# Attention scores of three row blocks per stretch instead of two, in a fused attention and MoE kernel

## The chip, the cores and the metric

The kernel runs on one core of a Trainium2 chip. The metric is device time in microseconds (us) of one execution. The kernel before was timed three times: median 813.93 us, lowest 813.37, highest 815.35.

The engines of a core are named as the profile names them: PE (matrix products; PEld is its loading of weights), DVE (vector work), ACT (exponentials and copies with a scale), POOL (vector work without access to the accumulation banks), SP (here it only issues transfers). PE writes into eight accumulation banks, each of 128 rows by 512 fp32 numbers, from which DVE and ACT read.

## The reference

`x` of 2048 rows by 640 is normalized row by row to `xn`. It feeds an attention with 32 heads of 192 over the last 512 rows of a cache, and a small MoE that picks two rows; the result is `x + s * g`.

```python
def _A_ref(x, k_cache, v_cache, wq, wo):
    ...
    q = (lambda x, *d: x.transpose(*d))((x @ wq).reshape(B, Sq, Hq, Dh), 0, 2, 1, 3)
    ...
    scores = jnp.einsum("bhqd,bhkd->bhqk", q, k) * (Dh ** -0.5)
    p = _softmax(scores, axis=-1)
    o = jnp.einsum("bhqk,bhkd->bhqd", p, v)
    return (lambda x, *d: x.transpose(*d))(o, 0, 2, 1, 3).reshape(B, Sq, Hq * Dh) @ wo
...
xn = _layernorm(x, axis=-1)
s = _A_ref(xn, A_k_cache, A_v_cache, A_wq, A_wo)
g = _silu(_B_ref(xn, B_w_r, B_w_gate, B_w_up, B_w_down))
return x + s * g
```

`_B_ref` finds the two rows with the largest `xn @ w_r`, runs them through a gated feed-forward layer, and adds the results to `xn` at these rows.

## The kernel before

**Loops.** The 32 heads are taken in 8 groups of 4, a group as two couples of heads (`pr`). The 2048 rows are taken in 4 blocks of 512 (`t5`). A step `i` is one group, one row block, one couple of heads; there are 64 steps. A step has four row blocks of 128, and one row block of 128 for one couple of heads is called a pair below: 256 pairs in all. The main loop runs over 128 stretches `k`, each with two pairs (`quad`, L310).

**One stretch**, in the order in which the code writes it; the code fixes each engine's order itself, and every engine works through its own list in that order, waiting where data or a buffer is missing:

- `quad`: scores of two pairs, four banks. A head's 192 columns are contracted in a full part of 128 rows and a rest of 64 rows. The four full products come first (L321, L322), then the rests (L327, L328), two at a time in the two halves of PE's rows.
- `row_max` (L339): DVE takes the negated maximum of each of the four score tiles.
- `exps` (L346): ACT takes the exponentials into `pexp`, with the row sums; SP then transposes `pexp` into `pT` by a transfer, once for both pairs (L352).
- `q_item` (L288): the q products of a later step in five matmuls of 512 columns each, copied out by ACT with a scale (L293). There are three per step.
- `o_item`: P V of stretch `k - 2`, eight matmuls of 192 columns per pair (L364), scaled by DVE with the reciprocal of the sums (L378). After the second pair SP transposes `o_sb` into `oT` (L382).
- `w_item`: the product of a 128-row block's o with wo for the group, six matmuls of 512 columns (L411) and six of 128 (L413), into the two banks of `w_ps`; DVE adds all 640 columns to `s_acc` (L419).
- `mid` and `bg`: lists of further work by stretch. They hold the MoE (products with `w_r` at L588, gates at L773 and L774), the normalization, and SP's loads of the next group.

The first 12 stretches and the last one are written out as token lists (`FIRST`, `LAST`), where each token is one of the items above.

**Banks.** `ps_sc` has four for scores, `ps_f` two for q, P V and small MoE products, `ps_w` two for `w_ps`.

**Rings.** `pexp` has 2 buffers, `pT` 4, `o_sb` 2, `oT` 3, each for the two pairs of a stretch.

**Transfers.** Nearly all are issued by SP in order; an issue that waits for its data holds up the ones behind it.

Of the kernel before, what the change touches and what calls it, by code (L numbers as in the profile page):

```python
# [21 lines left out]
def kernel(ctx, tc, A_x, A_k_cache, A_v_cache, A_wq, A_wo, B_x, B_w_r, B_w_gate, B_w_up, B_w_down, out):  # L22
    nc = tc.nc
# [44 lines left out]
    p_pool = pool("p", 2)  # L68
    pT_pool = pool("pT", 4)
    o_pool = pool("o", 2)  # L70
    oT_pool = pool("oT", 3)
# [10 lines left out]
    s_acc = big.tile([P, NTB, D], FP32, name="s_acc")  # L82

# [58 lines left out]
    warm_ps = ps_w.tile([P, W], FP32, name="warm_ps", tag="w_ps")  # L142
# [106 lines left out]
    def k_turn(copies):  # L249

        grp[0]["kT"] = kT_pool.tile([P, PAIRS, NJ, 3, P], BF16, name="kT")
        tp = ps_w.tile([P, NJ * 3, P], BF16, name="tp_k", tag="w_ps")
        kp = grp[0][("k", 0)].rearrange("p j h d -> p (j h d)")
        kT = grp[0]["kT"][:, 0].rearrange("p j c t -> p (j c) t")
        step = NJ * 3 // len(copies)
        for c in range(NJ * 3):
            nc.tensor.transpose(out=tp[:, c, :], in_=kp[:, c * P:(c + 1) * P], identity=ident)
        for q, copy in enumerate(copies):
            cs = slice(q * step, (q + 1) * step)
            copy(out=kT[:, cs], in_=tp[:, cs])  # L260
# [10 lines left out]
    NH = 2 * NS  # L271
    qT_of = {}
    pT_of = {}
    l_of = {}
    pe_of = {}
    o_of = {}
    oT_of = {}
# [32 lines left out]
    def quad(k):  # L310
        i, hf = divmod(k, 2)
        g, t5, pr = steps[i]
        qT = qT_of[i]
        kT = grp[g]["kT"]
        kp = kT[:, pr]
        tiles = []
        for u in range(2):
            ssl = slice((2 * hf + u) * P, (2 * hf + u + 1) * P)
            s0 = ps_sc.tile([P, W], FP32, name="s0", tag="sc")
            s1 = ps_sc.tile([P, W], FP32, name="s1", tag="sc")  # L320
            nc.tensor.matmul(s0, lhsT=qT[:, 0, ssl], rhs=kp[:, :, 0, :], start=True, stop=False)  # L321
            nc.tensor.matmul(s1, lhsT=qT[:, 2, ssl], rhs=kp[:, :, 2, :], start=True, stop=False)  # L322
            tiles.append((s0, s1))
        for u in range(2):
            ssl = slice((2 * hf + u) * P, (2 * hf + u + 1) * P)
            s0, s1 = tiles[u]
            nc.tensor.matmul(s0, lhsT=qT[0:64, 1, ssl], rhs=kp[0:64, :, 1, :], start=False, stop=True)  # L327
            nc.tensor.matmul(s1, lhsT=qT[64:128, 1, ssl], rhs=kp[64:128, :, 1, :], start=False, stop=True)  # L328
        return tiles
# [3 lines left out]
    def row_max(k, tiles, c):  # L333
        if c == 0:
            nm_of[k] = small.tile([P, 4], FP32, name="nm")
            l_of[k] = small.tile([P, 4], FP32, name="lsum", bufs=6)
            pT_of[k] = pT_pool.tile([P, 2, 2, NJ, P], BF16, name="pT")
            pe_of[k] = p_pool.tile([P, 2, 2, W], BF16, name="pexp")
        nc.vector.tensor_reduce(out=nm_of[k][:, c:c + 1], in_=tiles[c // 2][c % 2], axis=AX.X, op=ALU.max, negate=True)  # L339

    def exps(k, u, tiles):
        pexp = pe_of[k]
        nm = nm_of[k]
        for hh in range(2):
            c = 2 * u + hh
            nc.scalar.activation(out=pexp[:, u, hh, :], in_=tiles[u][hh], func=ACT.Exp, bias=nm[:, c:c + 1],  # L346
                                 scale=1.0, accum_out=l_of[k][:, c:c + 1])
        if k >= NH - 2:
            nc.sync.dma_start_transpose(out=pT_of[k][:, u].rearrange("p h j t -> p (h j) t"),
                                        in_=pexp[:, u].rearrange("p h k -> p (h k)"))  # L350
        elif u == 1:
            nc.sync.dma_start_transpose(out=pT_of[k].rearrange("p u h j t -> p (u h j) t"),  # L352
                                        in_=pexp.rearrange("p u h k -> p (u h k)"))

    def recip(k):
        nc.vector.reciprocal(out=l_of[k], in_=l_of[k])

    def o_products(k, u):
        i, hf = divmod(k, 2)
        g, t5, pr = steps[i]  # L360
        o_ps = f_tile([P, 2, Dh], FP32, "o_ps")
        for hh in range(2):
            for j in range(NJ):
                nc.tensor.matmul(o_ps[:, hh, :], lhsT=pT_of[k][:, u, hh, j, :], rhs=grp[g]["v"][:, 2 * pr + hh, j, :],  # L364
                                 start=(j == 0), stop=(j == NJ - 1))
        return o_ps

    def o_scaled(k, u, o_ps, act=False):
        i, hf = divmod(k, 2)
        g, t5, pr = steps[i]  # L370
        if u == 0:
            o_of[k] = o_pool.tile([P, 2, 2, Dh], BF16, name="o_sb")
        o_sb = o_of[k]
        if act:
            for hh in range(2):
                nc.scalar.activation(out=o_sb[:, u, hh], in_=o_ps[:, hh, :], func=ACT.Copy, scale=l_of[k][:, 2 * u + hh:2 * u + hh + 1])
        else:
            nc.vector.tensor_tensor(out=o_sb[:, u], in0=o_ps, in1=l_of[k][:, 2 * u:2 * u + 2].unsqueeze(2).to_broadcast([P, 2, Dh]), op=ALU.mult)  # L378
        if pr == 0 and u == 0:
            oT_of[(g, t5, hf)] = oT_pool.tile([P, PAIRS, 2, 3, P], BF16, name="oT")  # L380
        if u == 1 and k < NH - 2:
            nc.sync.dma_start_transpose(out=oT_of[(g, t5, hf)][:, pr].rearrange("p u c t -> p (u c) t"),  # L382
                                        in_=o_sb.rearrange("p u h d -> p (u h d)"))

    def o_item(k, u, act=False):
        return lambda: o_scaled(k, u, o_products(k, u), act)

    def o_turn(k):

        i, hf = divmod(k, 2)  # L390
        g, t5, pr = steps[i]
        tp = tail_banks[0].tile([P, 2, 3, P], BF16, name="tp_o", tag="t")
        for u in range(2):
            o2 = o_of[k][:, u].rearrange("p h d -> p (h d)")
            for c in range(3):
                nc.tensor.transpose(out=tp[:, u, c, :], in_=o2[:, c * P:(c + 1) * P], identity=ident)  # L396
        for u in range(2):
            nc.scalar.copy(out=oT_of[(g, t5, hf)][:, pr, u], in_=tp[:, u])
# [4 lines left out]
    def w_item(b, u, act=False):  # L403
        def item():
            g, t5, _ = steps[b * PAIRS]
            n = t5 * 4 + u
            oT = oT_of[(g, t5, u // 2)]
            wo_g = grp[g]["wo"]
            w_ps = ps_w.tile([P, D], FP32, name="w_ps")
            for c in range(CPG):  # L410
                nc.tensor.matmul(w_ps[:, 0:DA], lhsT=oT[:, c // 3, u % 2, c % 3, :], rhs=wo_g[:, c, 0:DA], start=(c == 0), stop=(c == CPG - 1))  # L411
            for c in range(CPG):
                nc.tensor.matmul(w_ps[:, DA:D], lhsT=oT[:, c // 3, u % 2, c % 3, :], rhs=wo_g[:, c, DA:D], start=(c == 0), stop=(c == CPG - 1))  # L413
            if g == 0 and act:
                nc.scalar.copy(out=s_acc[:, n, :], in_=w_ps)
            elif g == 0:
                nc.vector.tensor_copy(out=s_acc[:, n, :], in_=w_ps)
            elif g < NG - 1:
                nc.vector.tensor_tensor(out=s_acc[:, n, :], in0=s_acc[:, n, :], in1=w_ps, op=ALU.add)  # L419
            else:  # L420
                t = fin_pool["t"].tile([P, D], FP32, name="fin_t")
                o = fin_pool["o"].tile([P, D], BF16, name="fin_o")
                nc.vector.tensor_tensor(out=t, in0=w_ps, in1=xn[:, n, :], op=ALU.mult)
# [7 lines left out]
    mid = defaultdict(list)  # L431

# [40 lines left out]
    def first(token):  # L473
# [41 lines left out]
        elif op == "S":  # L515
            quads[n[0]] = quad(n[0])
# [8 lines left out]
        elif op == "O":  # L525
            o_item(*n, e == "a")()
        elif op == "W":
            w_item(*divmod(n[0], 4), act=e == "a")()
        else:
            for f in mid.pop(n[0], []) + bg.pop(n[0], []):  # L530
# [18 lines left out]
    for g in range(NG - 1):  # L549
        k0 = 16 * g  # L550
        k1 = k0 + (7 if g == 0 else 0)
        for dc in range(DC):
            bg[k1 + dc].append(lambda g=g, dc=dc: wq_piece(g + 1, dc, nc.sync))
        k1 = k0 + (8 if g == 0 else 5)
        for q in range(4):
            bg[k1 + q].append(lambda g=g, q=q: k_piece(g + 1, q // 2, q % 2, nc.sync))
            bg[k0 + (13 if g == 0 else 10) + q].append(lambda g=g, q=q: v_piece(g + 1, q, nc.sync))
        for c in range(CPG):
            bg[k0 + (15 if g == 0 else 9) + c].append(lambda g=g, c=c: wo_piece(g + 1, c, nc.sync))
        for pr in range(PAIRS):  # L560
            bg[k0 + (12 + 3 * pr if g == 0 else 10 + 2 * pr)].append(lambda g=g, pr=pr: k_transpose(g + 1, pr))
# [41 lines left out]
    def m_rows():  # L603
# [3 lines left out]
        M["rows"] = M["s"].tile([NTB, P], FP32, name="r_rows")  # L607
# [86 lines left out]
    def m_xsT():  # L694
# [4 lines left out]
        M["hT"] = M["s"].tile([P, FC, 32], BF16, name="hT")  # L699
# [89 lines left out]
    pieces = {0: (2, 2, 2, 2, 2), 1: (1, 1, 2, 2, 2, 2), 2: (2, 2, 2, 2, 2)}  # L789
    for fb, (k0, km) in enumerate(((37, 43), (44, 51), (52, 58))):  # L790
        q = 0
        for h, n in enumerate(pieces[fb]):
            for _ in range(n):
                bg[k0 + h].append(m_ffn_piece(fb, q))
                q += 1
# [3 lines left out]
    q = 0  # L799
    for h, n in enumerate((1, 1, 1, 2, 2, 2, 2, 1)):  # L800
        for _ in range(n):
            bg[59 + h].append(m_wd_piece(q))
            q += 1
# [148 lines left out]
```

## Time and profile before

| | before |
|---|---|
| median of three runs | 813.93 us |
| the profiled execution | 815.34 us |
| its span in the profile | 813.6 us |
| row maxima L339 | 512, mean 683 ns |
| exponentials L346 | 512, mean 689 ns |
| o scaling L378 | 249, mean 546 ns |
| adds of o wo L419 | 96, mean 821 ns |
| transposes pT (L352), median issue to landing | 4.8 us |
| transposes oT (L382), median issue to landing | 3.2 us |

The profile shows one execution. "Busy" of an engine is the time in which it executed something; for PE the durations of matmuls overlap, since a matmul of 512 columns is shown with some 380 ns while the next starts 216 ns later. "Idle before" is what an engine stood still ahead of a group of instructions, with the one that released it; "issue" means that the profile shows nothing it waited for. A transfer has two durations: SP's time to issue it, and the time from issue to landing.

### The profile page before, as it was taken

What the parts mean: (1) busy time and instruction counts of PE and PEld (TensorE: products, weight loads), DVE (VectorE), ACT (ScalarE), POOL (GpSimd) and SP (SyncE); (2) the same over time, 40 slices, a digit from 0 to 9 for tenths busy, and PEclk for the clock granted to TensorE, in tenths of its full rate; (3) what the DMA queues carried; (4) which work ended last, traced back from release to release, by engine and by line L of the source; (5) the groups of instructions that cost most, each with busy time, mean ns of one, the idle gap of its engine ahead of it and who ended that gap; (6) DMA issues with size and microseconds to landing.
All of it is one profiled execution on the core that took longest, in us unless ns stands there. A gap on an engine that the chain in (4) does not pass through costs nothing. (4 is left out here: it accounts for less than half of the span.)

```text
span 813.6 us, 15427 instructions
## 1 busy us (share of the span) xinstructions
PE 800.1 (98%) x5782; PEld 446.2 (55%) x5782; DVE 626.8 (77%) x1220; ACT 486.9 (60%) x1280; POOL 213.9 (26%) x174
## 2 busy tenths in 40 slices
PE   8899999999999999999999999999999999999997
PEld 4455555555555555555555555555555555555555
DVE  7988788887877766777767777678888877767886
ACT  5777655655655665556555655656676765655652
POOL 0112000000000000000001799999930001452533
PEclk9999999999999999999999999999999999999999
DMA  7998989999879999999999999889998989998985
GB/s 209 194 172 176 198 166 193 174 162 183 167 150 179 190 192 190 179 188 180 199 193 181 177 176 190 159 145 150 182 174 151 158 146 195 191 164 157 180 156 120
DMA packets 440555, 142.09 MB, mean 175 GB/s; under 512 B 413572, under 2 KB 440072, under 8 KB 440480
## 3 DMA queue, kind: packets, MB, share of 16 engines
q1 hardware_dynamic: 438720, 138.26, 91.1%
q0 software_dynamic: 816, 2.03, 1.0%
q8 instruction: 45, 0.74, 0.4%
q10 hardware_dynamic: 944, 0.82, 0.3%
q14 instruction: 30, 0.25, 0.1%
HBM read 39.98 MB, written 2.62 MB: 52 GB/s over the span
## 5 line engine op out<-in xcount | busy, mean ns | idle before, releaser
L346 ACT ACTIVATE pexp<-s,nm 128x512 bf16<-128x512 f32 x512 | 347.7, 689 | 255.9 <-DVE nm L339 157.4
L339 DVE TENSOR_REDUCE nm<-s 128x1 f32<-128x512 f32 x512 | 318.8, 683 | 55.5 <-PE s L328 54.5
L288 PE MATMUL q_ps<-xnT,wq_g 128*128 128x512 bf16 x945 | 235.1, 381 | 0.2 <-DVE o_sb L378 0.2
L364 PE MATMUL o_ps<-v_sb,pT 128*128 128x192 bf16 x2048 | 210.2, 246 | 2.5 <-DVE nm L339 1.1
L364 PEld LDWEIGHTS <-pT 128*128 128x128 bf16 x2048 | 172.9, 98 | 49.2 <-issue 4.9
L411 PE MATMUL w_ps<-wo_g,oT 128*128 128x512 bf16 x726 | 176.5, 379 | 0.0
L378 DVE TENSOR_TENSOR o_sb<-o_ps,lsum 128x384 bf16<-128x384 f32 x249 | 135.7, 546 | 47.2 <-PE o_ps L364 46.3
L288 PEld LDWEIGHTS <-wq_g 128*128 128x128 bf16 x945 | 80.4, 98 | 118.5 <-issue 49.8
L293 ACT ACTIVATE qT<-q_ps 128x512 bf16<-128x512 f32 x178 | 105.8, 595 | 38.6 <-PE q_ps L288 38.5
L419 DVE TENSOR_TENSOR s_acc<-s_acc,w_ps 128x640 f32<-128x640 f32 x96 | 78.8, 821 | 59.1 <-PE w_ps L413 58.9
L346 ACT ACTIVATION_READ_ACCUMULATOR pexp<-s,nm 128x1 f32 x512 | 105.9, 207 | 0.0
L411 PEld LDWEIGHTS <-oT 128*128 128x128 bf16 x726 | 69.1, 98 | 58.0 <-issue 0.4
L322 PE MATMUL s<-kT,qT 128*128 128x512 bf16 x256 | 97.1, 379 | 1.4 <-ACT pexp L346 0.9
L321 PE MATMUL s<-kT,qT 128*128 128x512 bf16 x256 | 97.2, 379 | 0.6 <-ACT pexp L346 0.6
L327 PE MATMUL s<-kT,qT 64*128 64x512 bf16 x256 | 77.1, 381 | 0.0
L328 PE MATMUL s<-kT,qT 64*128 64x512 bf16 x256 | 77.1, 381 | 0.0
L413 PEld LDWEIGHTS <-oT 128*128 128x128 bf16 x726 | 50.7, 98 | 28.5
L766 POOL TENSOR_SCALAR yh<-y_bc,oh 128x640 bf16<-128x640 bf16 x32 | 61.4, 1918 | 3.3 <-DMA y_bc<-y_d 1.8
L413 PE MATMUL w_ps<-wo_g,oT 128*128 128x128 bf16 x726 | 60.3, 219 | 0.0
L752 POOL DMA_DIRECT2D y<-yp x4 | 2.1, 525 | 220.1 <-ACT yp L746 219.9
L767 POOL TENSOR_TENSOR xn<-xn,yh 128x640 bf16<-128x640 bf16 x32 | 44.6, 1394 | 2.7
L327 PEld LDWEIGHTS <-qT 64*128 64x128 bf16 x256 | 14.2, 94 | 55.7 <-issue 54.8
(145 smaller groups left out, 399.8 us busy)
## 6 DMA issues: line engine op xcount, KB each, us to landing
wo_g<-in_A_wo_dram SPq DMA_DIRECT2D x48, 160.0 KB, 3.0
wq_g<-in_A_wq_dram SPq DMA_DIRECT2D x35, 192.0 KB, 3.0
k_raw<-in_A_k_cache_dram SPq DMA_DIRECT2D x32, 192.0 KB, 3.1
v_sb<-in_A_v_cache_dram SPq DMA_DIRECT2D x32, 192.0 KB, 2.7
x_fin<-in_A_x_dram SPq DMA_DIRECT2D x16, 160.0 KB, 2.9
pT<-pexp SPq DMA_TRANSPOSE x130, 4.8
oT<-o_sb SPq DMA_TRANSPOSE x126, 3.2
wgu<-in_B_w_gate_dram SPq DMA_DIRECT2D x15, 128.0 KB, 2.9
```

Of the source, the lines that this page charges most:

```text
L288: nc.tensor.matmul(q_ps, lhsT=grp[g]["wq"][:, dc, col0:col0 + P], rhs=xnT[:, t5 * 4:(t5 + 1) * 4, dc, :], start=(dc == 0), stop=(dc == DC ...
L293: nc.scalar.activation(out=qT_of[i][:, c, :], in_=q_ps, func=ACT.Copy, scale=scale)
L321: nc.tensor.matmul(s0, lhsT=qT[:, 0, ssl], rhs=kp[:, :, 0, :], start=True, stop=False)
L322: nc.tensor.matmul(s1, lhsT=qT[:, 2, ssl], rhs=kp[:, :, 2, :], start=True, stop=False)
L327: nc.tensor.matmul(s0, lhsT=qT[0:64, 1, ssl], rhs=kp[0:64, :, 1, :], start=False, stop=True)
L339: nc.vector.tensor_reduce(out=nm_of[k][:, c:c + 1], in_=tiles[c // 2][c % 2], axis=AX.X, op=ALU.max, negate=True)
L346: nc.scalar.activation(out=pexp[:, u, hh, :], in_=tiles[u][hh], func=ACT.Exp, bias=nm[:, c:c + 1], scale=1.0, accum_out=l_of[k][:, c:c + 1])
L364: nc.tensor.matmul(o_ps[:, hh, :], lhsT=pT_of[k][:, u, hh, j, :], rhs=grp[g]["v"][:, 2 * pr + hh, j, :], start=(j == 0), stop=(j == NJ - 1))
L378: nc.vector.tensor_tensor(out=o_sb[:, u], in0=o_ps, in1=l_of[k][:, 2 * u:2 * u + 2].unsqueeze(2).to_broadcast([P, 2, Dh]), op=ALU.mult)
L411: nc.tensor.matmul(w_ps[:, 0:DA], lhsT=oT[:, c // 3, u % 2, c % 3, :], rhs=wo_g[:, c, 0:DA], start=(c == 0), stop=(c == CPG - 1))
L413: nc.tensor.matmul(w_ps[:, DA:D], lhsT=oT[:, c // 3, u % 2, c % 3, :], rhs=wo_g[:, c, DA:D], start=(c == 0), stop=(c == CPG - 1))
L419: nc.vector.tensor_tensor(out=s_acc[:, n, :], in0=s_acc[:, n, :], in1=w_ps, op=ALU.add)
```

## The change

**Scores in threes.** The first 12 stretches stay as they are. From pair 24 on a stretch (`units`) holds three pairs; 77 such follow, and a last one with a single pair. The full products of the second and third pair are written first, into the four banks of `ps_sc`, then those of the first pair, into the two banks of the o wo product; then follow the half-height products of all three, the first pair's first.

**Banks of o wo.** The two banks are now two tiles for the whole run (`w_banks`). o wo is computed in two halves of 320 columns, one in each bank, and each half is evacuated by itself.

**Rings of pairs.** `pexp` becomes a ring of 5 pairs (two twos that alternate, and one place for every third pair), `pT` of 6 pairs, `o_sb` of 6, `oT` of 15.

**Three transposes a stretch.** One for the first two pairs' `pexp` after their exponentials, one for the third's, one for the three pairs' `o_sb`.

**Order.** A stretch follows `STRETCH`; P V in it is that of the three pairs that are four before its own. o wo of an item comes when the last pair of the stretch reaches 14 + 2 times the item's number, alternately one and two per stretch. `LAST` is written anew for a stretch of three and one of one, with one transposition of o by PE for one pair at a time (six instructions fewer).

**Loads.** SP's loads have a list of their own (`loads`), run at the end of a stretch, and their stretches are moved.

```diff
+    RP, RO, RT = 6, 6, 15
+    p_ring = big.tile([P, 5, 2, W], BF16, name="pexp")
+    pT_ring = big.tile([P, RP, 2, NJ, P], BF16, name="pT")
+    o_ring = big.tile([P, RO, 2, Dh], BF16, name="o_sb")
+    oT_ring = big.tile([P, RT, 3, P], BF16, name="oT")
...
+    HEAD = 12
+    units = [[2 * k, 2 * k + 1] for k in range(HEAD)]
+    while units[-1][-1] < NM - 2:
+        units.append([units[-1][-1] + 1 + a for a in range(3)])
+    units.append([NM - 1])
...
+    def scores(U):
+
+        ms = units[U]
+        tiles = {}
+        for m in ms[1:] + ms[:1] if len(ms) == 3 else ms:
...
+            if len(ms) == 3 and m == ms[0]:
+                s0, s1 = w_banks()
+            else:
+                s0 = ps_sc.tile([P, W], FP32, name="s0", tag="sc")
+                s1 = ps_sc.tile([P, W], FP32, name="s1", tag="sc")
+            qT, kp = qT_of[m // 4], grp[g]["kT"][:, pr]
             nc.tensor.matmul(s0, lhsT=qT[:, 0, ssl], rhs=kp[:, :, 0, :], start=True, stop=False)
             nc.tensor.matmul(s1, lhsT=qT[:, 2, ssl], rhs=kp[:, :, 2, :], start=True, stop=False)
+            tiles[m] = (s0, s1)
+        for m in ms:
...
             nc.tensor.matmul(s0, lhsT=qT[0:64, 1, ssl], rhs=kp[0:64, :, 1, :], start=False, stop=True)
             nc.tensor.matmul(s1, lhsT=qT[64:128, 1, ssl], rhs=kp[64:128, :, 1, :], start=False, stop=True)
...
+        slot = 2 if a == 2 else 3 * (U % 2) + a
...
+        n = 1 if a == 2 or U >= NU - 3 else 2
+        if a % n == n - 1:
+            s0, m0 = slot + 1 - n, (m + 1 - n) % RP
+            nc.sync.dma_start_transpose(out=pT_ring[:, m0:m0 + n].rearrange("p u h j t -> p (u h j) t"),
+                                        in_=p_ring[:, s0:s0 + n].rearrange("p u h k -> p (u h k)"))
...
+            for h, w_ps in enumerate(w_banks()):
+                cs = slice(h * HD, (h + 1) * HD)
+                w_products(b, u, w_ps, cs, cs.start)
...
+                    nc.vector.tensor_tensor(out=s_acc[:, n, cs], in0=s_acc[:, n, cs], in1=w_ps[:, 0:HD], op=ALU.add)
...
+    for g in range(2, NG - 1):
+        group_loads(g + 1, range(16 * g, 16 * g + 5), range(16 * g + 4, 16 * g + 8), (16 * g + 7, 16 * g + 9),
+                    range(16 * g + 8, 16 * g + 12), [16 * g + a for a in (8, 10, 12, 13, 14, 15)])
...
+    pieces = {0: (33, (2, 2, 2, 1, 2, 1)), 1: (42, (2, 2, 2, 2, 2)), 2: (49, (2, 2, 2, 1, 2, 1))}
...
+    STRETCH = "M0 M1 R O1 E0 q1 M2 M3 E1 O1 M4 M5 E2 W1 m q1 n W q O b l".split()
...
+        os_ = [o_item(m) for m in range(no, ms[0] - 1)] + [lambda no=no, U=U: o_turned(list(range(no, units[U][0] - 1)))]
+        while 14 + 2 * nw <= ms[-1]:
+            ws.append(w_item(*divmod(nw, 4)))
+            nw += 1
```

In `STRETCH`, M is a row maximum, E the exponentials of a pair, R the reciprocal of the sums of the stretch before, O1 P V of one pair with its scaling, q1 one q item, W1 one o wo item, m, n and b the lists of further work, l the loads; a letter without a number stands for all that is left.

More of the change, by code (lines that the diff above doesn't have):

```diff
@@ L308, in q_first, with w_banks @@
             nc.scalar.activation(out=evac, in_=q_ps, func=ACT.Copy, scale=scale)
[L310 to L320, printed above, removed]
+    def w_banks():
+        if not wb:
+            wb.extend(ps_w.tile([P, W], FP32, name=f"w_{c}", tag=f"w{c}") for c in range(2))
+        return wb
@@ L327, in quad, with row_max @@
             nc.tensor.matmul(s0, lhsT=qT[0:64, 1, ssl], rhs=kp[0:64, :, 1, :], start=False, stop=True)
             nc.tensor.matmul(s1, lhsT=qT[64:128, 1, ssl], rhs=kp[64:128, :, 1, :], start=False, stop=True)
-        return tiles
+        return [tiles[m] for m in ms]
     nm_of = {}
-    def row_max(k, tiles, c):
+    def row_max(U, tiles, c):
         if c == 0:
[L335 to L339, printed above, removed]
@@ L379, in o_scaled @@
[L379 to L394, printed above, removed]
+            nc.vector.tensor_tensor(out=o_sb, in0=o_ps, in1=ls.unsqueeze(2).to_broadcast([P, 2, Dh]), op=ALU.mult)
@@ L395, in o_turn, with w_products @@
             for c in range(3):
                 nc.tensor.transpose(out=tp[:, u, c, :], in_=o2[:, c * P:(c + 1) * P], identity=ident)
-        for u in range(2):
-            nc.scalar.copy(out=oT_of[(g, t5, hf)][:, pr, u], in_=tp[:, u])
+        for u, m in enumerate(ms):
+            nc.scalar.copy(out=oT_ring[:, (m + 1) % RT], in_=tp[:, u])
+    def w_products(b, u, w_ps, part, off=0):
+        wo_g = grp[steps[b * PAIRS][0]]["wo"]
+        for c in range(CPG):
+            nc.tensor.matmul(w_ps[:, part.start - off:part.stop - off], lhsT=oT_ring[:, (8 * b + 4 * (c // 3) + u + 1) % RT, c % 3, :],
+                             rhs=wo_g[:, c, part], start=(c == 0), stop=(c == CPG - 1))
@@ L406, in item @@
             n = t5 * 4 + u
[L407 to L423, printed above, removed]
+            for h, w_ps in enumerate(w_banks()):
+                cs = slice(h * HD, (h + 1) * HD)
+                w_products(b, u, w_ps, cs, cs.start)
+                if g == 0 and act:
+                    nc.scalar.copy(out=s_acc[:, n, cs], in_=w_ps[:, 0:HD])
+                elif g == 0:
+                    nc.vector.tensor_copy(out=s_acc[:, n, cs], in_=w_ps[:, 0:HD])
+                elif g < NG - 1:
+                    nc.vector.tensor_tensor(out=s_acc[:, n, cs], in0=s_acc[:, n, cs], in1=w_ps[:, 0:HD], op=ALU.add)
+                else:
+                    if h == 0:
+                        t = fin_pool["t"].tile([P, D], FP32, name="fin_t")
+                        o = fin_pool["o"].tile([P, D], BF16, name="fin_o")
+                    nc.vector.tensor_tensor(out=t[:, cs], in0=w_ps[:, 0:HD], in1=xn[:, n, cs], op=ALU.mult)
+            if g == NG - 1:
                 nc.vector.tensor_tensor(out=o, in0=t, in1=s_acc[:, n, :], op=ALU.add)
@@ L431 @@
     mid = defaultdict(list)
+    loads = defaultdict(list)
     def ln_parts(t5):
@@ L515, in first @@
         elif op == "S":
-            quads[n[0]] = quad(n[0])
+            quads[n[0]] = scores(n[0])
         elif op == "M":
@@ L798 @@
         bg[km + 1].append(turn)
[L799 to L803, printed above, removed]
+    for q, a in enumerate((57, 58, 59, 59, 60, 60, 61, 61, 62, 62, 63, 64)):
+        loads[a].append(m_wd_piece(q))
     bg[60].append(m_sig)
@@ L856, with q_until @@
-    last_quad = []
+    def q_until(s):
+        a, r = divmod(s - 1, 4)
+        return min(3 * NS, 3 * (HEAD // 2 + 2) if s == 0 else 3 * (HEAD // 2 + 3) + 9 * a + 2 * r)
+    nq, no, nw = 3 * (HEAD // 2 + 1), 2 * (HEAD - 2), HEAD // 2
+    for U in range(HEAD, NU - 2):
+        ms = units[U]
+        qs = [q_item(*divmod(n, 3)) for n in range(nq, q_until(U - HEAD))]
+        nq += len(qs)
+        os_ = [o_item(m) for m in range(no, ms[0] - 1)] + [lambda no=no, U=U: o_turned(list(range(no, units[U][0] - 1)))]
+        no = ms[0] - 1
+        ws = []
+        while 14 + 2 * nw <= ms[-1]:
+            ws.append(w_item(*divmod(nw, 4)))
+            nw += 1
+        ks = [m // 2 for m in ms if m % 2 == 0]
+        todo = {"q": qs, "O": os_, "W": ws, "m": mid.pop(ks[0], []), "b": bg.pop(ks[-1], []),
+                "n": bg.pop(ks[0], []) + mid.pop(ks[-1], []) if len(ks) > 1 else [],
+                "l": [f for k in ks for f in loads.pop(k, [])]}
+        tiles = scores(U)
+        for token in STRETCH:
+            if token[0] == "M":
+                row_max(U, tiles, int(token[1]))
+            elif token[0] == "E":
+                exps(U, int(token[1]), tiles)
+            elif token[0] == "R":
+                if U > HEAD:
+                    recip(U - 1)
+            elif token[1:] == "":
+                while todo[token]:
+                    todo[token].pop(0)()
+            else:
+                for f in todo[token[0]][:int(token[1])]:
+                    todo[token[0]].pop(0)()
+        assert not any(todo.values())
@@ L905, in last @@
                     tail_sb["t", tok] = fin_pool["t"].tile([P, D], FP32, name="fin_t")
-                nc.vector.tensor_tensor(out=tail_sb["t", tok][:, cs], in0=tail_ps[key], in1=xn[:, tok, cs], op=ALU.mult)
+                for h in range(2) if half is None else (int(half),):
+                    hs = slice(h * HD, (h + 1) * HD)
+                    nc.vector.tensor_tensor(out=tail_sb["t", tok][:, hs], in0=tail_ps[key][h], in1=xn[:, tok, hs], op=ALU.mult)
             else:
@@ L920 @@
         last(token)
-    assert not bg and not mid
+    assert not bg and not mid and not loads
 _INS = ['A_x', 'A_k_cache', 'A_v_cache', 'A_wq', 'A_wo', 'B_x', 'B_w_r', 'B_w_gate', 'B_w_up', 'B_w_down']
```

199 lines of the change are left out of this document (92 added, 107 removed).

## The prediction

> **What bounds the kernel now.** I read the page's busy shares first, then the waits, then the timeline of one stretch of the loop, then the transposes' times to landing.
>
> ```profile
> PE 800.1 (98%) x5782; PEld 446.2 (55%) x5782; DVE 626.8 (77%) x1220; ACT 486.9 (60%) x1280; POOL 213.9 (26%) x174
> ...
> q1 hardware_dynamic: 438720, 138.26, 91.1%
> ```
> ```profile
> PEld L327 <- issue: 54.8, 127, 0.9
> ...
> PEld L288 <- issue: 49.8, 118, 0.4
> ...
> PEld L364 <- DMA pT<-pexp: 4.3, 7, 1.6
> ```
> ```profile
> 400.77 0.38 PE L321 MATMUL s<-kT,qT 128*128 128x512 bf16 x1
> ...
> 400.98 0.38 PE L322 MATMUL s<-kT,qT 128*128 128x512 bf16 x1
> 401.29 0.09 PEld L327 LDWEIGHTS <-qT 64*128 64x128 bf16 x1 [0.42 <-issue]
> ...
> 401.30 0.39 PE L327 MATMUL s<-kT,qT 64*128 64x512 bf16 x1
> 401.30 0.39 PE L328 MATMUL s<-kT,qT 64*128 64x512 bf16 x1
> ...
> 401.52 0.38 PE L327 MATMUL s<-kT,qT 64*128 64x512 bf16 x1
> 401.52 0.38 PE L328 MATMUL s<-kT,qT 64*128 64x512 bf16 x1
> 401.72 1.29 DVE L339 TENSOR_REDUCE nm<-s 128x1 f32<-128x512 f32 x2 [0.62 <-PE s L328]
> 401.83 0.76 PEld L288 LDWEIGHTS <-wq_g 128*128 128x128 bf16 x5 [0.42 <-issue]
> ```
>
> PE is busy 98%, but matmul durations overlap, so I take the distances from start to start in the trace's records. Their medians are 216 ns for a matmul of 512 columns, 83 for 192 (P V), 56 for 128, and 223 for a pair of 64-row matmuls (L327 and L328 start 3 ns apart and count once). Nearly every distance after 60 us is one of these: PE streams without pause. Two distances stand out. From the last full matmul of a quad (L322) to its first half-height pair (L327) it is 312 ns instead of 216, 128 times; from the last pair (L328) to the next full matmul it is 308 instead of 223. In the timeline these are 400.98 to 401.30 and 401.52 to 401.83; the weight load there is "idle 0.42", and the waits list has that 127 and 118 times, waiting for nothing but issue. So each quad pays 96 + 85 = about **182 ns to change from full to half height and back**. True waits of PE after 60 us come to some 5 us, about 2.1 of them at transposed probabilities (pT) that had not landed, the longest 1.31 us at 308 us.
>
> The Trainium skill ("Perfetto Trace Analysis", section Identifying the Most-Contended Engine) calls matmul busy time a poor measure of headroom and prefers the weight-load share, here 55%, which would leave PE much room. The start distances speak against it here.
>
> **The change, part by part.** (1) Scores in threes. Twelve opening stretches keep two pairs (a "pair" is 128 rows of two heads); then come 77 of three and one of one: 90 stretches for 128. Full and half-height matmuls stay 256 x 2 each. That removes 38 changes there and back: 38 x 0.182 = **-6.9 us**, on the engine that sets the end.
>
> (2) o wo in two halves of 320 columns instead of 512 + 128. PE: 6 x (216 + 56) = 1.63 us; a 320-column matmul takes 136 ns (L900's rows), 12 x 136 = 1.63: **0**. DVE pays more: one 128x640 add is 821 ns, a 128x320 row (L906) 492, so +0.16 us an item, about +17 us over the run, less 38 reciprocals of 171 ns (-6.5). DVE goes from 77% to some 79%; PE hides it while DVE is on time.
>
> (3) Six PE transposes fewer in the tail: 6 x 56 ns = **-0.3 us**.
>
> (4) The order inside a stretch, by durations of the trace. Steps between starts: row maximum 0.60 us, exp 0.66, o scaling 0.53, q copy 0.48. From the last half-height start to the maximum is 0.42 us; from a maximum's end to its exp 0.19. PE of one stretch: scores 6 x 0.216 + 3 x 0.223 + 0.18 = 2.15; P V 24 x 0.083 = 1.98; q 1.08 each; o wo 1.63 each. In cycles of four there are 3 q + 1 o wo (9.0 us), 2 + 2 (9.55), 2 + 1 (7.9), 2 + 2 (9.55). The shortest, from its start: maxima at 1.81 and 2.41, first o scaling 3.10, maxima 3.63 and 4.23, second scaling 4.83, maxima 5.36 and 5.96; exps at 2.68, 3.34, 4.57, 5.23, 6.23, 6.89, ending 7.58. The banks these free last are wanted by the third score matmul of the next stretch at 7.92 + 0.43 = 8.35: 0.7 us to spare. The first o wo ends at 6.18, its adds start when DVE ends the maxima (6.56), and the first bank is free at 7.05. In 2 + 2 stretches the second o wo wants it at 7.26: 0.2 us to spare. So the plain stretch streams: **0**.
>
> (5) Where DVE and ACT carry more. Gates (L773 740 ns on ACT, L774 826 on DVE) come 16 times within 11 stretches: in the 5 with two, the second o wo's adds follow the first gate and the next scores wait for the second bank about 0.3 us; the second gate pushes the first o scaling back, and the second P V block's buffer comes 0.4 late. 5 x 0.7 = 3.7 at most, 0 if DVE catches up; I take **+1.5**. The 16 r products (816 + 84 ns) fit by the same table. In the opening, six o wo evacuations split: one ACT copy of 640 takes 692 ns, two halves perhaps 0.2 more; 0 to 1, taken **+0.3**. In the tail each second o wo waits for the same two banks; my table gives about 1.4 us of waits where the trace of before has 1.0 (0.22 + 0.75): -0.5 to +1.5, taken **+0.4**.
>
> (6) pT, and SP's queue. Half the 2.1 us and more of waits should go, since the loads are spread thinner: 0 to -2.1, taken **-1.5**. But the time that a transposition has shrinks. Before, from a quad's last exp to its P V are 8.7 to 10.7 us. After, the transpose of two pairs is issued at the second pair's exps (5.9) and its P V comes 3.9 us into the next stretch: 5.8 us in the shortest, 6.8 and 7.4 in the others. Its landing:
>
> ```profile
> L352 SPq DMA_TRANSPOSE pT<-pexp x126: 1318/2561/4542, 18.8 to 785.9; - x126
> ...
> DMA to landing us min/median/max: 4.3/4.8/8.1
> ```
> The columns are shortest, median and longest: SP's time to issue, and issue to landing. Of these landings 18% exceed 5.8 us, by 0.09 on average over all, 1% exceed 6.8. With 19 + 19 + 39 stretches that is 19 x 0.09 + 58 x 0.01 = 2.2 us at most if SP issues at once; 0 if the thinner loads shorten them. SP issues at once if it is free: its oT transpose (1.27 us for two pairs, so 1.9 for three) ends about 2.7 us into the stretch, loads of 0.42 to 0.58 us each may follow until 5.9, room for six. By the order of SP's instructions most stretches have one to three; about a dozen, near the MoE weights, have six or seven, or a kT transpose with three or more loads, and may run over by up to 1 us, which the 5.8 against 4.8 us mostly covers. With 12 x 0.1 for these I take **+1.5**, 3.4 at the bad end. The third pair's pT has 12 us against 3.6 (L349's rows). The single third slot of the ring (12 us from issue round to reuse less a landing) has room too. Number and bytes of transposes are about the same (261 for 256).
>
> **Sum**: -6.9 - 0.3 + 1.5 + 0.3 + 0.4 - 1.5 + 1.5 = **-5.0 us**. The profiled execution took 815.34 (span 813.6 and 1.7 around it), the slow end of the three runs (813.37 to 815.35): 810.3 against it; against the median 813.93, **808.9**. With every unknown at its good end (-6.9 - 0.3 - 0.5 - 2.1) it is 804.1, at its bad end (-7.2 + 3.7 + 1 + 1.5 + 3.4) 816.3.
>
> **Rivals.** *B, slower: pT late behind SP's loads.* SP issued for 68 to 96% of each 50 us after the start, and in before a pT left up to 4.8 us after its exps. Were that delay the same after, exps to landing would exceed 5.8, 6.8 and 7.4 us by 0.67, 0.33 and 0.22 on average: 19 x 0.67 + 19 x 0.33 + 39 x 0.22 = 27.6 us, less the 1.5 counted: **835**. It decides from about 1 us of delay (4.8 + 1 = the 5.8 window). For it: SP's work per pair is unchanged. Against it: before, the late ones came in runs of stretches that each had two to four loads; after, a stretch of six or seven is followed by one of one to three (4.0 + 1.9 + 7 x 0.5 = 9.4 us of issuing, then 7.4), so no delay is handed on. The Trainium skill ("Perfetto Trace Analysis", What "DMA-bound" means) names an issuing sequencer of solid DMA slices as a bound of its own; by it B would hold near 400 us, where SP stood at 96%.
>
> *C, no change: the two shared banks.* If the first o wo's adds come 0.2 us later than my table, each of 38 two-o-wo stretches waits; 0.15 to 0.2 us beyond the margin each, 6 to 8 us: **about 815 to 817**. For it: 0.2 us is the thinnest margin, and before the two banks held nothing else. Against it: PE also runs late then, and the margin returns. The same page's section Matmuls asks that independent groups rotate through different banks; here scores and o wo no longer do.
>
> *D, PE is not the bound* (the weight-load rule): removing drains changes nothing, **814**. The start distances leave it little.
>
> **Chances.** Forecast (804 to 811) 0.70; B 0.13 (some of it near 820 only); C 0.13; D 0.02; a miss below 804, 0.02. About 0.3% (2.4 us) is what a measurement of this kernel tells from no change: faster than 811.5 0.72, within 0.14, slower than 816.4 0.14. The range runs from all costs absent (804) to the middle of C, 816.
>
> **What would show it.** Right: distances of 312 and 308 ns 90 times instead of 128, "PEld ... issue" falling to about 70% in total, PE's other distances unchanged. B: PEld or PE at P V waiting for DMA pT well above 4.3 us. C: PE at o wo or at the third pair's scores waiting for DVE's adds. The gates: waits between 560 and 655 us. Wrong altogether: half-height changes that cost more after three pairs, or a DVE share well above 80%.

## The result and the profile after

The changed kernel takes **808.55 us** (median of six runs, 807.38 to 810.42) against 813.75 for the kernel before in the same six rounds: a ratio of 0.9935, 95% interval 0.9915 to 0.9954. The forecast was 808.9. The profiled execution took 807.38, its span is 805.6.

The page of the changed kernel, its heads and two of its groups:

```profile
PE 790.8 (98%) x5776; PEld 483.2 (60%) x5776; DVE 624.1 (77%) x1303; ACT 500.2 (62%) x1281; POOL 217.4 (27%) x175
...
q1 hardware_dynamic: 439936, 138.79, 90.0%
...
L437 DVE TENSOR_TENSOR s_acc<-s_acc,w 128x320 f32<-128x320 f32 x192 | 86.3, 479 | 28.1 <-PE w L419 28.0
```

PE is again busy 98%, now for 9 us less. DVE did not rise: its 192 adds are busy 86.3 us, 7.5 more than the 96 that they replace, and the reciprocals, 38 fewer, take 5.9 us less (16.0 instead of 21.9).

The waits of the changed kernel (us in total, times, longest):

```profile
PEld L343 <- issue: 38.4, 89, 0.9
PEld L378 <- issue: 36.6, 85, 0.9
...
PEld L378 <- DMA pT<-pexp: 8.0, 11, 1.2
...
PE o_ps L378 <- DMA pT<-pexp: 3.2, 7, 0.8
```

The two rows that wait for nothing but issue are the changes to half height and back: 89 and 85 times, 75 us together, where before they were 127 and 118 times and 104.6 us (72%). The waits for pT are longer than before: that part of the gain went the other way.

The timeline of the changed kernel, PE in one stretch of three:

```profile
595.48 0.38 PE L336 MATMUL w<-kT,qT 128*128 128x512 bf16 x1
595.79 0.39 PE L343 MATMUL w<-kT,qT 64*128 64x512 bf16 x1
...
596.02 0.38 PE L343 MATMUL s<-kT,qT 64*128 64x512 bf16 x1
...
596.23 0.38 PE L343 MATMUL s<-kT,qT 64*128 64x512 bf16 x1
...
596.54 0.83 PE L378 MATMUL o_ps<-v_sb,pT 128*128 128x192 bf16 x8
```

One way in (595.48 to 595.79, 0.31 us), three pairs of half-height products, one way out (596.23 to 596.54, 0.31): what a stretch of two paid, for three. A part of the price stands one step behind each change. Half-height pairs start 0.23 us apart right after the way in (595.79 to 596.02: 226 ns, from the trace) and 0.21 apart after that (216 ns): they stream at 216 ns like the full products. The first step behind a way out is 10 ns long in the same way, 93 ns instead of 83 in P V here, 226 instead of 216 in the q products of before. So one way costs 96 + 10 ns, and there and back **0.21 us**.

All distances from one PE start to the next, sorted by what they are, in the two profiled executions (us). A wait of P V is put to pT or to the gates by what was done last ahead of it:

| | before | after | difference |
|---|---|---|---|
| beyond the streaming time at changes of height (256, then 180), the step behind each included | 27.1 | 19.0 | -8.1 |
| waits of P V for pT after 60 us, ahead of the tail | 2.1 | 3.1 | +1.0 |
| waits of P V behind the gates (560 to 655 us) | 1.0 | 0.9 | -0.1 |
| other waits in that stretch of time | 1.4 | 0.6 | -0.8 |
| waits in the last 30 us | 1.0 | 1.9 | +0.9 |
| waits before 60 us | 8.3 | 8.3 | 0.0 |
| opening products (L144, L146) beyond 216 ns | 2.6 | 1.7 | -0.9 |
| rest (six transposes of 56 ns fewer, and small differences) | | | 0.0 |
| span | 813.6 | 805.6 | -8.0 |

The profiles differ by 8.0 us, the medians by 5.2. The opening products run their first 12 (before) or 8 (after) starts at about 426 ns, a number that went from 7 to 14 over all the profiles of this study, whatever the kernel; 0.9 us of the 8.0 is that. The profiled execution of before, 815.34, also lies 1.6 above its median, and that of after 1.2 below; the last two runs look into it.

### The profile page after: what moved, and what is told of

Read it like the earlier page. It is cut to its first block, busy times and chain, and to the rows that moved or that the text cites. A ratio compares the mean times of both kernels' runs of the same rounds, so it can differ in the third digit from the quotient of the medians.

```text
span 805.6 us, 15848 instructions
## 1 busy us (share of the span) xinstructions
PE 790.8 (98%) x5776; PEld 483.2 (60%) x5776; DVE 624.1 (77%) x1303; ACT 500.2 (62%) x1281; POOL 217.4 (27%) x175
## 4 chain that ended last, share of the span: by engine, by line
PE 89%; DMA 4%; DVE 3%; ACT 2%; issue 1%; DVEq 0%; SPq 0%; ACTq 0%
PE w L419 24%; PE q_ps L294 23%; PE o_ps L378 20%; PE s L336 4%; PE s L335 4%; PE s L343 4%; DMA pT<-pexp 4%; PE w L343 3%; PE w L335 2%; PE w L336 2%; DVE nm L353 2%; ACT pexp L361 1%; PE warm_ps L146 1%; DVE o_sb L393 0%; PE tp L267 0%
## 5 line engine op out<-in xcount | busy, mean ns | idle before, releaser
L361 ACT ACTIVATE pexp<-s,nm 128x512 bf16<-128x512 f32 x358 | 242.3, 684 | 14.9 <-DVE nm L353 10.5
L361 ACT ACTIVATE pexp<-w,nm 128x512 bf16<-128x512 f32 x154 | 104.5, 683 | 229.7 <-DVE nm L353 229.6
L353 DVE TENSOR_REDUCE nm<-s 128x1 f32<-128x512 f32 x358 | 228.6, 679 | 4.5 <-PE s L344 3.7
L419 PE MATMUL w<-wo_g,oT 128*128 128x320 bf16 x1500 | 224.2, 299 | 0.0
L419 PEld LDWEIGHTS <-oT 128*128 128x128 bf16 x1536 | 148.6, 98 | 58.7 <-issue 0.9
L353 DVE TENSOR_REDUCE nm<-w 128x1 f32<-128x512 f32 x154 | 99.1, 685 | 66.1 <-PE w L344 66.1
L437 DVE TENSOR_TENSOR s_acc<-s_acc,w 128x320 f32<-128x320 f32 x192 | 86.3, 479 | 28.1 <-PE w L419 28.0
L361 ACT ACTIVATION_READ_ACCUMULATOR pexp<-s,nm 128x1 f32 x358 | 72.0, 201 | 0.0
L336 PE MATMUL s<-kT,qT 128*128 128x512 bf16 x179 | 67.8, 379 | 1.4 <-ACT pexp L361 0.9
L335 PE MATMUL s<-kT,qT 128*128 128x512 bf16 x179 | 67.9, 379 | 0.6 <-ACT pexp L361 0.6
L343 PE MATMUL s<-kT,qT 64*128 64x512 bf16 x179 | 53.2, 377 | 0.0
L344 PE MATMUL s<-kT,qT 64*128 64x512 bf16 x179 | 53.2, 377 | 0.0
```

The lines of the kernel that those rows point to most:

```text
L353: nc.vector.tensor_reduce(out=nm_of[U][:, c:c + 1], in_=tiles[c // 2][c % 2], axis=AX.X, op=ALU.max, negate=True)
L361: nc.scalar.activation(out=p_ring[:, slot, hh, :], in_=tiles[a][hh], func=ACT.Exp, bias=nm_of[U][:, c:c + 1], scale=1.0, accum_out=l_of[U] ...
L419: nc.tensor.matmul(w_ps[:, part.start - off:part.stop - off], lhsT=oT_ring[:, (8 * b + 4 * (c // 3) + u + 1) % RT, c % 3, :], rhs=wo_g[:, ...
L437: nc.vector.tensor_tensor(out=s_acc[:, n, cs], in0=s_acc[:, n, cs], in1=w_ps[:, 0:HD], op=ALU.add)
```

## The experiments

The theory: PE streams and sets the end; the gain is 38 changes of height there and back, less the waits that the new order adds, above all for pT. The rivals: the gain comes from the longer lag, the finer banks or the spread loads; the shared banks or SP's queue decide. Each run was timed in five rounds with the kernel before on the same chip, except the last two, which are one execution each.

**x1_two_height_changes.** The changed kernel with one more change of height in each stretch of three.

```diff
-        for m in ms[1:] + ms[:1] if len(ms) == 3 else ms:
...
-        for m in ms:
...
+            full(ms[1])
+            full(ms[0])
+            rest(ms[0])
+            full(ms[2])
+            rest(ms[1])
+            rest(ms[2])
```

> The changed kernel, but in each of the 77 stretches of three the first pair's half-height products come right after its full ones, the other two pairs' later: two changes of height there and back per stretch instead of one, everything else as in the changed kernel. Theory (the gain is changes of height saved): 77 x 0.182 = 14.0 us more than the changed kernel's 808.55, about 822.6, with 167 distances of about 312 and 308 ns each in place of 90. Rival (the gain came with the longer lag, the rings and the loads, and the changes are hidden or cheaper when they come close together): between 808 and 813.

Measured: 823.25 us, ratio to before 1.0123 (1.0103 to 1.0143); the changed kernel at its ratio would be 807.6 on this chip, so 15.6 more; the profiled spans differ by 15.9. Its timeline:

```profile
403.22 0.38 PE L337 MATMUL w<-kT,qT 128*128 128x512 bf16 x1
403.53 0.09 PEld L345 LDWEIGHTS <-qT 64*128 64x128 bf16 x1 [0.42 <-issue]
403.53 0.39 PE L345 MATMUL w<-kT,qT 64*128 64x512 bf16 x1
...
403.85 0.39 PE L336 MATMUL s<-kT,qT 128*128 128x512 bf16 x1
...
404.08 0.38 PE L337 MATMUL s<-kT,qT 128*128 128x512 bf16 x1
404.39 0.09 PEld L345 LDWEIGHTS <-qT 64*128 64x128 bf16 x1 [0.42 <-issue]
```

The weight load stands 0.42 us ahead of each way in, twice in one stretch. There are 167 ways in instead of 90, and what the changes cost, with the step behind each, is 35.4 us against 19.0: 16.4 us for 77 more, 0.21 each (`full` writes a pair's full products, `rest` its half-height ones). Of the rest, P V waits 2.3 us less than in the changed kernel, five scores wait 0.18 us each for the second bank beside the gates, and the opening products take 1.0 us more; together that is 16.0, against 15.9 by the spans. At this price the 38 changes that the changed kernel saves are 8.1 us, more than its whole gain: they are the gain.

**x2_halves_alone.** The kernel before with o wo in halves alone.

```diff
-            w_ps = ps_w.tile([P, D], FP32, name="w_ps")
...
+            for h in range(2):
+                w_ps = ps_w.tile([P, W], FP32, name=f"w_{h}", tag=f"w{h}")
+                cs = slice(h * HD, (h + 1) * HD)
```

> The kernel before with one part of the change alone: o wo in two halves of 320 columns in two single banks, each evacuated by itself. Theory (DVE's extra 0.16 us an item is hidden by PE): 813.75 within 1.5 us, DVE busy some 17 us more. Rival (finer banks let PE run ahead and are part of the gain): 2 us or more below, 811; rival on the other side (DVE's extra work shows): 2 us or more above.

Measured: 812.57 us, ratio 0.9996 (0.9984 to 1.0007), DVE busy 639.0 us instead of 626.8. No gain and no loss; PE hides DVE's 12 us.

**x3_old_loads.** The changed kernel with the loads where they were.

```diff
...
-    group_loads(2, (19, 20, 21, 22, 23), (22, 23, 24, 25), (25, 27), (26, 27, 28, 29), (26, 28, 30, 31, 32, 33))
-    for g in range(2, NG - 1):
-        group_loads(g + 1, range(16 * g, 16 * g + 5), range(16 * g + 4, 16 * g + 8), (16 * g + 7, 16 * g + 9),
-                    range(16 * g + 8, 16 * g + 12), [16 * g + a for a in (8, 10, 12, 13, 14, 15)])
...
+    for g in range(1, NG - 1):
+        group_loads(g + 1, range(16 * g, 16 * g + 5), range(16 * g + 5, 16 * g + 9), (16 * g + 10, 16 * g + 12),
+                    range(16 * g + 10, 16 * g + 14), range(16 * g + 9, 16 * g + 15))
```

The MoE's loads and products go back to their stretches in the same way.

> The changed kernel with SP's loads and the MoE's feed-forward items in the stretches that they had before. Theory (the spread of the loads is worth little by itself; it limits pT's waits): 1 to 4 us slower than the changed kernel, 809.5 to 812.5, and PE's and PEld's waits for pT of 11.2 us together rise to 14 or more. Rival (the spread does nothing): 808.55 within 1 us and the same waits. Rival (the spread is the change's real gain): 813 or more.

Measured: 810.59 us, ratio 0.9972 (0.9962 to 0.9982): 0.0037 of before, 3.0 us, more than the changed kernel. The waits for pT rise to 12.1 (PEld) and 4.6 (PE), and what PE loses at P V for pT ahead of the tail rises from 3.1 to 6.2 us. The spread pays for what the shorter window costs, and is not the gain.

**x4_single_transposes.** The changed kernel with a transpose per pair.

```diff
-        n = 1 if a == 2 or U >= NU - 3 else 2
+        n = 1 if U >= HEAD else 2
```

> The changed kernel with a transpose for every pair right after its exponentials, in place of one for the first two pairs and one for the third. The first pair's pT, which P V needs first, is then issued 1.3 us earlier and is half as long. Theory (the 3.8 us of P V waits left are a matter of when the transpose of two lands): they go, 804.5 to 806.5. Rival (SP's issuing is the bound and a transpose costs it 1.24 us whatever its size): 77 x 1.2 us more on SP, loads are late, waits grow, 809 or more.

Measured: 805.61 us, ratio 0.9914 (0.9896 to 0.9932), 1.9 us below the changed kernel run beside the next ones (0.9937). The intervals of the two ratios overlap; it is the waits that tell them apart. The transposes pT, of the changed kernel and then of this one (SP's time to issue, and issue to landing):

```profile
L366 SPq DMA_TRANSPOSE pT<-pexp x169: 1231/1805/4481, 17.9 to 790.8; - x169
...
DMA to landing us min/median/max: 3.1/4.3/7.7
```
```profile
L366 SPq DMA_TRANSPOSE pT<-pexp x244: 1231/1251/4369, 17.6 to 787.6; - x122
...
  PEld L378: 3.4, 5
  PE o_ps L378: 1.3, 2
DMA to landing us min/median/max: 3.0/3.4/7.7
```

What PE loses at P V for pT ahead of the tail falls from 3.1 to 0.3 us (the 3.8 of the expectation are 2.9 of that and 0.9 behind the gates). The 1.5 us that P V still waits there (0.83, 0.53 and 0.15) stand behind the gates, not behind a transpose. The rival that counted 1.24 us of SP for each of 75 more transposes is out: SP issued for 615 us in all instead of 613.

**x5_single_and_tail.** As x4, and SP relieved in the tail.

```diff
+            if int(n[0]) == 250:
+                o_turned([249, 250])
...
-                nc.sync.dma_start(out=out_v[:, tok, cs], in_=tail_sb["o", tok][:, cs])
+                (nc.gpsimd if tok < 12 and op == "g" else nc.sync).dma_start(out=out_v[:, tok, cs], in_=tail_sb["o", tok][:, cs])
```

> The changed kernel with a transpose per pair, and besides in the tail: the results of five row blocks are sent out by POOL's queue instead of SP's, and two o transposes are joined, so that SP reaches the last two pT transposes earlier. Theory (the two waits of P V in the tail, 0.65 and 0.96 us in the changed kernel, are SP's queue): they go, 1.0 to 1.9 us less than with single transposes alone (805.61): 803.7 to 804.6. Rival (the waits are the transposes' own time, or POOL's transfers end later): no change, 805 to 806.5.

Measured: 804.13 us, ratio 0.9889 (0.9866 to 0.9912). SP in the tail of the changed kernel:

```profile
784.39 1.25 SPq L366 DMA_TRANSPOSE pT<-pexp  x1
785.73 1.22 SPq L399 DMA_TRANSPOSE oT<-o_sb  x1
787.04 1.26 SPq L366 DMA_TRANSPOSE pT<-pexp  x1
788.39 1.01 SPq L955 DMA_DIRECT2D out_dram<-fin_o  x2
789.50 1.18 SPq L399 DMA_TRANSPOSE oT<-o_sb  x1
790.77 1.26 SPq L366 DMA_TRANSPOSE pT<-pexp  x1
```

The last pT leaves at 790.77, though its exponentials ended at 786.93: two results and an o transpose stood ahead of it. Moved away, the two waits are gone; lost time in the last 30 us is 0.7 instead of 1.9. This is the fastest kernel of the study, below x4 and the changed kernel.

**x6_before_single.** The kernel before with a transpose per pair.

```diff
-        if k >= NH - 2:
+        if k >= NH - 2 or k >= 12:
```

> The kernel before with a transpose of pT for every pair instead of one for two, from the thirteenth stretch on. Theory (before, P V has 8.7 to 10.7 us for a transpose and only SP's backlog made it late; single ones take SP about as long or a little longer): no change, within 1.5 us of before, waits for pT between 2 and 6 us. Rival (single transposes are a gain of their own, apart from the threes): 2 us or more faster than before. Rival (1.24 us of SP for each): SP falls behind, 2 us or more slower.

Measured: 811.84 us, ratio 0.9988 (0.9975 to 1.0001), and no wait of P V that PE shows after 60 us ahead of the tail, fewer than the 2 to 6 us expected. Some 0.9 us, at the edge of the interval: the kernel before had that much to gain from single transposes, the changed one about twice that.

**x7_wo_back_to_back.** The changed kernel with the second o wo right behind the first.

```diff
-    STRETCH = "M0 M1 R O1 E0 q1 M2 M3 E1 O1 M4 M5 E2 W1 m q1 n W q O b l".split()
+    STRETCH = "M0 M1 R O1 E0 q1 M2 M3 E1 O1 M4 M5 E2 W m q1 n q O b l".split()
```

> The changed kernel, but in a stretch with two o wo items the second follows the first at once, without the q product between them. Theory (the two banks are shared and the second item waits until DVE has added the first: the table has the banks free at 7.05 us and PE at the second item at 6.18): about 0.75 us in each of 38 stretches, 28 us, 832 to 840, all of it as waits of PE at o wo for DVE. Rival (the wait is made up later, as PE has slack elsewhere or DVE adds earlier): 808 to 815.

Measured: 843.23 us, ratio 1.0371 (1.0347 to 1.0395), 35.4 above the changed kernel beside it, more than expected. Its waits:

```profile
PEld L378 <- issue: 43.4, 91, 1.8
...
PEld L419 <- issue: 30.8, 39, 1.0
...
PE w L419 <- DVE s_acc L437: 19.6, 32, 0.8
...
PE o_ps L378 <- DVE o_sb L393: 5.7, 5, 1.5
```

PE's waits outside P V are 29.2 us longer, 0.77 for each of 38 second items: the size from the table. The other 6 us are at P V, whose banks DVE frees later; the expectation had not counted them. So the shared banks can decide, and the q product between the two items is what keeps them from it.

**r8_changed_again.** The changed kernel beside x5 to x7.

> The changed kernel as it is, beside the three others on the same chip: 0.9935 of before, and about 0.25% above the one with single transposes.

Measured: 807.82 us, ratio 0.9937 (0.9913 to 0.9961). Ahead of the tail P V waits 3.1 us for pT and 0.9 behind the gates, as in the first profile; single transposes (x4) are 0.0023 of before, 1.9 us, below it.

**r9_before_again and r10_before_again.** The kernel before, two more profiles.

> The kernel before once more, for a second profile. If its profiled execution of 815.34 us was a slow one, as its place above the median suggests, this one shows a span of 810.5 to 812.5 and fewer than 3.1 us of waits of P V after the opening, with the changes of height at 24.1 us as before. If the waits are fixed by the schedule, they are 3.1 us again at the same times.

> The same a third time: whether the waits of P V come at the same places and in the same size in each execution.

Measured: 814.43 and 811.76 us, spans 812.7 and 810.0. Changes of height cost 27.1 us in both, as in the first profile (the 24.1 of the expectation leaves out the step behind each). What differs are the waits of P V and the opening products. For pT, P V waited 2.1 us in the first profile and 1.6 and 0.4 here (the wait at 308 us is 1.31, 1.03 and 0.25); behind the gates it waited 1.0, 0.4 and 0.4; and 12, 14 and 7 opening products ran at about 426 ns. So the waits come largely at the same places, not in the same size. The span of r9, 812.7, lies just above the one expected, with 14 slow opening products.

## Why the prediction was right, step by step

**(1) Scores in threes, -6.9.** Right in place and cause; the size was 1.1 us short. Measured -8.1, and 16.4 us for the 77 changes that x1 adds: 0.21 us each, not 0.182. The step took the 223 ns between two half-height pairs for their streaming time. A stretch of two has only one such distance, and it is the one behind the way in; the third pair shows 216. So 10 ns of the way in were counted as streaming, the same 10 ns were taken off the way out (308 - 223), and the 10 ns behind the way out were not looked for.

**(2) o wo in halves, 0.** Right (x2). DVE's extra work was mis-sized: +17 us and 79% were forecast, 12 us were measured alone in x2 (79%), and in the changed kernel DVE stays at 77%. An add is 479 ns, not 492, and follows the one before after 0.40.

**(3) Six transposes, -0.3.** The products are gone; too small to be seen by itself.

**(4) The table of a stretch, 0.** It held to about 0.1 us. DVE and PE in a stretch of the changed kernel with two o wo items, which starts at 594.40:

```profile
596.22 1.29 DVE L353 TENSOR_REDUCE nm<-w 128x1 f32<-128x512 f32 x2 [0.20 <-PE w L344]
...
597.52 0.51 DVE L393 TENSOR_TENSOR o_sb<-o_ps,lsum 128x384 bf16<-128x384 f32 x1
...
599.63 1.28 DVE L353 TENSOR_REDUCE nm<-s 128x1 f32<-128x512 f32 x2
600.83 0.87 DVE L437 TENSOR_TENSOR s_acc<-s_acc,w 128x320 f32<-128x320 f32 x2
603.12 0.82 DVE L802 SCALAR_TENSOR_TENSOR xn<-tz,xn 128x640 bf16<-128x640 f32 x1 [1.42 <-ACT tz L801]
603.86 0.88 DVE L437 TENSOR_TENSOR s_acc<-s_acc,w 128x320 f32<-128x320 f32 x2
```
```profile
601.66 1.79 PE L419 MATMUL w<-wo_g,oT 128*128 128x320 bf16 x12
...
603.96 0.38 PE L335 MATMUL s<-kT,qT 128*128 128x512 bf16 x1
...
604.82 0.38 PE L335 MATMUL w<-kT,qT 128*128 128x512 bf16 x1
605.03 0.38 PE L336 MATMUL w<-kT,qT 128*128 128x512 bf16 x1
```

First maximum at 1.82 (table 1.81), first o scaling 3.12 (3.10), last maxima 5.23 (5.36), adds 6.43 (6.56), second o wo 7.26 (7.26).

**(5) Gates +1.5, opening +0.3, tail +0.4.** The gates' path was right, its count was not. The second bank did not run late: this is the same stretch, with a gate ahead of the second adds, and they end at 604.74 while the scores take that bank at 605.03, 0.3 us to spare where the step had them wait 0.3. The other half of the step, the second P V block behind a late o scaling, came once, at 644.7 us, and cost 0.83 us; in r8, x3, x4 and x5 it came at the same place, with 0.83 each time. P V there waits for DVE, and DVE was late by one gate of 1.77 us:

```profile
PE o_ps L378 <- DVE o_sb L393: 0.7, 1, 0.7
```
```profile
L802 DVE SCALAR_TENSOR_TENSOR xn<-tz,xn x16: 807/825/1771, 551.0 to 641.2; 128x640 bf16<-128x640 f32 x16
```

In the kernel before, the same instruction goes up to 2.04 us, and the two P V waits of its first profile that come 4.5 us after its longest gates are 1.0 us in all (that the gates cause them is read from the order alone):

```profile
L774 DVE SCALAR_TENSOR_TENSOR xn<-tz,xn x16: 814/826/2035, 561.3 to 653.0; 128x640 bf16<-128x640 f32 x16
```

So the gates cost 0.9 us after and 0.4 to 1.0 before, where the step had +1.5; it went by the median of 826 ns and left the long ones out. The opening cost 0.0. The tail cost 0.9 rather than 0.4, and not at the shared banks that the step named: both large waits were for pT behind SP's queue (x5).

**(6) pT and SP.** The two terms, -1.5 for the old waits and +1.5 for new ones, cancelled in the sum. Against the mean of the three profiles of before (2.1, 1.6 and 0.4: 1.4 us) the changed kernel's 3.1, in both its profiles, are +1.7. Such a wait:

```profile
277.18 0.57 SPq L117 DMA_DIRECT2D v_sb<-in_A_v_cache_dram  x1
277.80 0.43 SPq L122 DMA_DIRECT2D wo_g<-in_A_wo_dram  x1
278.28 0.90 SPq L695 DMA_DIRECT2D wgu<-in_B_w_gate_dram  x2
279.22 0.43 SPq L117 DMA_DIRECT2D v_sb<-in_A_v_cache_dram  x1
279.70 0.91 SPq L695 DMA_DIRECT2D wgu<-in_B_w_gate_dram  x2
280.71 4.80 SPq L366 DMA_TRANSPOSE pT<-pexp  x2
```
```profile
288.01 0.83 PE L378 MATMUL o_ps<-v_sb,pT 128*128 128x192 bf16 x8 [0.38 <-DMA pT<-pexp]
```

SP issued seven loads without a pause and then the transposes; the first of the two took 3.45 us to issue, landed 7.25 after its issue, and PE lost 0.54. The step had this mechanism and put its new cost at 0 to 3.4. By its two terms 2.1 us should have stood after as before; 3.1 did, 1.0 more. The other 0.7 is that it read the old waits from one execution, one with more of them than the next two, so that less was there to win.

**The sum.** Against the mean of three profiles of before: -8.1 and -0.3 by the changes of height and the transposes, -0.8 by other waits, -0.6 by the opening products, +1.7 by pT, +0.3 by the gates and +0.9 by the tail make -6.9; the spans say -6.5 (812.1 to 805.6). The medians say -5.2. The changed kernel's two profiled executions lie 1.2 and 0.4 us below its medians, and what its slower executions spend is in no profile. The forecast of -5.0 had the right main term, and it was luck that it met the medians so closely: the change itself was worth 1.1 us more than counted, gates and opening cost 1.5 less, other waits fell by 0.8 that were not counted, and against these stand 1.7 for pT and 0.5 in the tail that were not counted either.

**The rivals.** B (pT late behind the loads) was real in kind and came to 3.1 us ahead of the tail and 1.6 in it, of 27.6; x3, with the loads as before, shows where it begins (6.2 us ahead of the tail). C (the shared banks) did not happen: in the stretch of step (4) the first bank is free at 601.30 and wanted at 601.66, and behind the gate the second is free 0.3 us early; x7 takes the margin away and pays 35 us. D (PE is not the bound) is out by x1: PE's added time came out in the span. That x1 holds also settles the weight-load measure: at 55 and 60% of weight loading, there was no room on PE in either kernel. The longer lag from the scores to P V has no run of its own; the 0.8 us of other waits are the most that it, with all else, can have brought. The Trainium skill ("TensorEngine Tiling (Array Packing)", section Key Properties) says that a change of tiling mode drains the engine. No view here shows the draining itself; what the traces show is 0.21 us there and back, and a weight load held back by 0.42 us at each change.

## What to carry to other kernels

Where PE streams, sort its start-to-start distances by kind: a step that comes at every change between full and half-height products, however small, is worth grouping away, and its count times its price is the forecast. Look one step past the change for the price too, and check the streaming time where nothing changes. Then lay one stretch out as a table from durations and spacings and look at the thinnest margin, since an order that fits by 0.2 us is worth tens of microseconds against one that does not. Read waits for transfers from more than one execution before counting on them, and give the first part that is needed a transfer of its own.

## What the runs showed of the hardware

A change between full and half-height products costs 96 ns at the change and 10 ns at the step behind it, each way (medians of 256 and 180 changes in the two kernels, 334 in x1).

SP's time to issue pT's transposes goes with how much is transposed, not with their number: 322 us for 130 in the kernel before, 325 for 169 in the changed one, 334 for 244 in x4. The shortest times are alike (1.23 us for one pair, 1.32 for two), but the medians are not: 1.25 in x4, nearly all of one pair, and 2.56 for two pairs in before. Two transposes of half the size cost SP about the same as the double one, and the first lands earlier. The o transposes differ: their median is 1.27 us for two pairs and 1.34 for three. By this, three o transposes in one save SP time, which the prediction had not seen (it took 1.9): SP issued for 613 us in the changed kernel and 663 in the one before. Why the two kinds differ is not shown.

A gate on DVE (L774 before, L802 after) takes 0.82 us, but 0.9 to 2.0 at some places. In the twelve profiles all 38 gates over 0.86 us ran beside an instruction of POOL; of the 154 shorter ones 34 did. In the changed kernel the one of 1.77 us began at 641.16, with an add of POOL (L850) running from 640.85 for 1.40 us. No run moved POOL's work away, so that POOL is the cause is not shown.
